# First level of a sum over eight shifts by accumulating DMA, in a pre-layernorm block with local dilated attention and a gated ReLU feed-forward

## Chip, cores and metric

One core of one Trainium2 chip. The metric is device time in microseconds (us) of one execution. Before the change it is 209.4 us, the median of 13 runs (208.21 to 209.86).

TensorE (PE) multiplies matrices into PSUM, VectorE (DVE) does elementwise work, ScalarE (ACT) does activations and copies out of PSUM. GpSimd (POOL) and SyncE (SP) can issue DMAs. Each engine takes its instructions in the order in which they were written: one that waits holds up all behind it on that engine.

## What is computed

`x` is 2048 rows by 512, in bf16. Cut to what matters:

```python
# attention: 32 heads of 16; row s sees rows s, s-2, ..., s-14
qkv = layernorm(x) @ wqkv
logits[s, w] = (q[s] . k[s - 2*w]) * scale        # w = 0..7, masked where s - 2*w < 0
attn = softmax(logits over w)
o[s] = sum over w of attn[s, w] * v[s - 2*w]
h = x + o @ wo
# feed-forward, F = 1376
n = layernorm(h)
out = h + (relu(n @ W_gate) * (n @ W_up)) @ W_down
```

## The kernel before

Everything is held transposed where it can be: the 512 features on 4 x 128 partitions, the rows along the free axis. The 2048 rows are cut into four **chunks** of 512 (`tk` = 0 to 3), and each chunk goes through the same stages.

1. *First layernorm*: statistics on DVE (L390, L393), logarithm and exponential for the reciprocal root on ACT, then four normalized `row` tiles. The table `LNA` says which engine makes them: for chunk 0 DVE (L425), for chunks 1, 2 and 3 ACT (L422), which needs one small DVE step more (L411). PE transposes them (L456), ACT copies them out (L470).
2. *Projections* q, k, v: L502 on PE, copied out by ACT (L510).
3. *Scores*: products of q with four shifted views of k at a time on DVE (L549, four a chunk, 128x4096 each), summed over each head by PE (L555); exponential on ACT (L571), denominator (L588) and its reciprocal (L591, L594), each weight spread over the partitions of its head by PE (L616) and copied out by ACT (L622) into a `big` tile of 8 x 512 columns. In chunks 1 to 3 the weights are normalized before this (L603), in chunk 0 at the end (L644).
4. *Weighted sum*: for each of the four feature groups `t`, DVE multiplies the spread weights by eight shifted views of v into a `big` tile (L637) and adds the eight shifts in a tree of three levels: 4 + 4, then 2 + 2 (both L640), then 1 + 1 (L640 in chunk 0, L663 in the others).
5. *Output projection*: L683 on PE, and the residual. For chunk 0 (`RPE = (0,)`) PE adds x through an identity matmul (L686), and ACT copies the sum out with a row total (L692). For the other chunks DVE adds it (L694).
6. *Second layernorm* (L352, L360, L400, L407, L425), transposes as above, then *feed-forward*: up and gate matmuls (L721), copies (L725, L728), their product on DVE (L741), the down projection (L758), residual (L769) and the output DMA (L773).

The stages of different chunks overlap. Their order is not that of the loops: every step is given to a small planner (`Plan`) with an engine, a duration, what it depends on and the buffers that it takes. `order()` repeatedly looks, on each engine, at the steps that could start first by those durations (within a margin of 0.3 us on DVE), and takes the one with the smallest number in the table `RANK`. The steps are then written out in order of planned start. `RANK` is a hand-kept list with one number for each step.

Buffers that the weighted sum shares: five `big` tiles serve the score products, the spread weights and the trees; nine `quad` tiles hold transposed rows; eight PSUM banks serve everything that PE writes.

After the setup GpSimd has nothing to do. Input and weight DMAs go from SP and ACT, output DMAs from SP.

Of the kernel before, what the change touches and what calls it, by code (L numbers as in the profile page):

```python
# [13 lines left out]
ALU = mybir.AluOpType  # L14
# [1 line left out]


RANK = [
    4, 1, 5, 2, 0, 3, 47, 6, 7, 29, 171, 229, 201, 272, 727, 10, 12, 8, 11, 14,
    17, 23, 28, 32, 20, 26, 31, 16, 18, 21, 24, 27, 34, 37, 9, 13, 15, 19, 22, 25,  # L20
    30, 33, 35, 40, 45, 42, 46, 57, 38, 43, 49, 52, 56, 61, 59, 66, 70, 78, 63, 68,
    67, 74, 75, 99, 84, 157, 136, 167, 73, 180, 72, 94, 88, 101, 109, 114, 65, 83, 87, 95,
    102, 122, 165, 209, 212, 121, 131, 129, 149, 127, 134, 144, 139, 153, 151, 156, 179, 210, 222, 226,
    164, 174, 196, 206, 224, 169, 183, 200, 216, 219, 187, 202, 208, 213, 218, 237, 247, 240, 249, 230,
    238, 233, 239, 254, 267, 255, 263, 242, 258, 243, 260, 270, 273, 282, 292, 276, 283, 295, 278, 286,
    280, 287, 291, 310, 320, 319, 327, 313, 323, 316, 324, 331, 308, 333, 302, 329, 305, 332, 299, 318,
    336, 345, 361, 352, 364, 337, 360, 330, 356, 366, 328, 351, 335, 353, 342, 354, 322, 349, 359, 358,
    381, 368, 389, 363, 384, 365, 387, 393, 355, 391, 348, 382, 399, 395, 417, 709, 733, 429, 434, 716,
    736, 371, 403, 706, 732, 406, 413, 714, 735, 44, 51, 36, 50, 39, 48, 41, 53, 55, 60, 64,
    76, 81, 71, 80, 86, 82, 85, 69, 77, 89, 105, 112, 97, 107, 108, 116, 96, 104, 125, 133,  # L30
    130, 137, 128, 135, 113, 126, 143, 344, 161, 271, 140, 338, 154, 312, 124, 141, 146, 152, 192, 132,
    147, 150, 163, 195, 205, 234, 245, 264, 252, 296, 306, 301, 307, 304, 265, 284, 300, 288, 298, 350,
    362, 370, 374, 309, 321, 339, 347, 340, 367, 372, 376, 314, 326, 334, 377, 386, 397, 390, 402, 383,
    388, 380, 385, 401, 404, 405, 407, 396, 400, 392, 398, 410, 414, 420, 426, 416, 422, 430, 419, 423,
    424, 427, 432, 440, 467, 455, 476, 454, 471, 464, 480, 486, 449, 463, 437, 457, 441, 460, 448, 461,
    466, 468, 481, 439, 465, 472, 484, 451, 469, 489, 446, 473, 458, 487, 443, 477, 462, 488, 491, 475,
    501, 479, 502, 485, 507, 482, 504, 525, 492, 512, 490, 508, 528, 495, 531, 718, 737, 521, 550, 722,
    740, 516, 535, 720, 738, 547, 552, 724, 741, 62, 90, 58, 92, 54, 91, 79, 93, 98, 100, 110,
    155, 159, 145, 158, 162, 142, 148, 119, 138, 160, 198, 220, 181, 217, 176, 214, 184, 223, 166, 228,
    172, 232, 170, 231, 186, 236, 189, 444, 173, 456, 203, 379, 168, 450, 235, 244, 259, 268, 315, 227,  # L40
    256, 257, 279, 317, 325, 343, 346, 357, 409, 369, 408, 418, 411, 394, 412, 428, 436, 435, 425, 447,
    478, 494, 498, 459, 470, 493, 497, 438, 442, 445, 452, 453, 474, 483, 496, 500, 505, 511, 519, 503,
    510, 506, 515, 509, 513, 522, 523, 514, 517, 518, 520, 527, 532, 537, 541, 538, 544, 549, 542, 545,
    534, 539, 551, 585, 606, 554, 583, 572, 603, 569, 600, 612, 564, 579, 568, 581, 555, 575, 560, 576,
    584, 574, 595, 570, 594, 562, 598, 566, 591, 602, 559, 588, 578, 608, 557, 586, 601, 611, 614, 589,
    624, 605, 636, 596, 621, 593, 619, 639, 580, 641, 610, 643, 648, 625, 655, 729, 745, 615, 650, 726,
    742, 637, 654, 728, 743, 633, 657, 730, 746, 111, 118, 106, 117, 115, 123, 103, 120, 175, 177, 178,
    190, 197, 185, 193, 204, 188, 194, 182, 191, 199, 248, 262, 211, 250, 207, 241, 215, 253, 221, 275,
    274, 290, 225, 277, 246, 281, 289, 499, 251, 556, 261, 565, 269, 561, 266, 294, 293, 341, 375, 285,
    303, 297, 311, 373, 378, 415, 421, 431, 524, 433, 530, 533, 536, 526, 529, 540, 548, 546, 543, 553,  # L50
    573, 582, 590, 558, 577, 587, 597, 567, 592, 599, 607, 563, 571, 604, 609, 620, 631, 613, 618, 616,
    623, 617, 628, 634, 635, 622, 626, 627, 629, 630, 632, 638, 640, 651, 652, 645, 649, 656, 642, 646,
    644, 647, 653, 662, 676, 658, 670, 667, 679, 660, 673, 690, 674, 693, 688, 696, 668, 681, 664, 683,
    699, 669, 692, 672, 687, 685, 689, 680, 686, 697, 665, 678, 677, 684, 661, 675, 659, 671, 694, 663,
    701, 666, 703, 682, 710, 691, 705, 712, 695, 704, 698, 708, 711, 707, 717, 734, 749, 700, 719, 739,
    750, 702, 715, 731, 747, 713, 721, 744, 751, 723, 725, 748, 752,
]


# [33 lines left out]
class Plan:  # L93
# [9 lines left out]
    def add(self, key, *a, **k):  # L103
        op = Op(*a, **k)
        op.key = key
        op.seq = len(self.ops)
        if RANK:
            op.prio = RANK[op.seq]
        self.ops.append(op)
        for b in set(op.take) | set(op.use):  # L110
            b.left += 1
        return op
# [57 lines left out]
def kernel(  # L170
# [11 lines left out]
    nc = tc.nc  # L182
# [121 lines left out]
    add = plan.add  # L304


    PESUM = ()
    NWARM = 48
    DMAT = ()

    EARLY = (1, 2, 3)

    RPE, OPE = (0,), ()

    MERGE = ()

    BCN = 4

    LNA = ((0, 1, 1, 1), (0, 0, 0, 0))


    MM, TP = 0.2165, 0.07
# [155 lines left out]
    def f_warm(wb=wb):  # L478
        for _ in range(NWARM):
            nc.tensor.matmul(wb.t[:, 0:P], lhsT=warm[:], rhs=warm[:], start=True, stop=True)  # L480
# [4 lines left out]
    for tk in range(NCK):  # L485
# [143 lines left out]
        for t in range(NT):  # L629
            mt = Buf(big_s)  # L630
            tpr = apr + 3 + t

            def f_mu(t=t, ab=ab, mt=mt, s0=s0):
                vb = vT[:, t, PADL + s0: PADL + s0 + CS]
                v8 = bass.AP(tensor=vb.tensor, offset=vb.offset,
                             ap=[list(vb.ap[0]), [-DIL, W]] + [list(y) for y in vb.ap[1:]])
                V.tensor_tensor(out=mt.t[:], in0=ab.t[:], in1=v8, op=ALU.mult)  # L637

            def f_a(n, mt):
                V.tensor_tensor(out=mt.t[:, 0:n, :], in0=mt.t[:, 0:n, :], in1=mt.t[:, n:2 * n, :],  # L640
                                op=ALU.add)

            def f_om(t=t, mt=mt, rc=rc, OT=OT):
                V.tensor_tensor(out=OT.t[:, t, :], in0=mt.t[:, 0, :], in1=rc.t[:], op=ALU.mult)  # L644

            m = add(("mu%d" % t, tk), "DVE", D40, f_mu, abd + [vd[t], kdone.get(("v", tk - 1, t))], tpr,
                    take=[mt], use=[ab], lat=DL)
            if (tk, t) in PESUM:
                u = Buf(od_s)

                def f_ac(mt=mt, u=u):
                    for w in range(W):
                        nc.tensor.matmul(u.t[:], lhsT=identity[:], rhs=mt.t[:, w, :],
                                         start=(w == 0), stop=(w == W - 1))

                def f_om(t=t, u=u, rc=rc, OT=OT):
                    V.tensor_tensor(out=OT.t[:, t, :], in0=u.t[:], in1=rc.t[:], op=ALU.mult)

                m = add(("ac%d" % t, tk), "PE", 8 * MM, f_ac, [m], tpr, take=[u], use=[mt], lat=PEL)
                oev[t] = add(("om%d" % t, tk), "DVE", D5, f_om, [m, rcd], tpr, take=[OT], use=[u, rc], lat=DL)  # L660
                continue
            def f_al(t=t, mt=mt, OT=OT):
                V.tensor_tensor(out=OT.t[:, t, :], in0=mt.t[:, 0, :], in1=mt.t[:, 1, :], op=ALU.add)  # L663

            for n, du in ((4, D20), (2, D10), (1, D2)):
                f = lambda n=n, mt=mt, f=f_a: f(n, mt)
                if n == 1 and tk in EARLY:
                    oev[t] = add(("tree%d" % t, tk), "DVE", du, f_al, [m], tpr, take=[OT], use=[mt], lat=DL)
                else:
                    m = add(("tree%d" % t, tk), "DVE", du, f, [m], tpr, use=[mt], lat=0.03)  # L670
            if tk not in EARLY:
                oev[t] = add(("om%d" % t, tk), "DVE", D2, f_om, [m, rcd], tpr, take=[OT], use=[mt, rc], lat=DL)
# [37 lines left out]
        for f0 in range(0, NFT, 2):  # L710
# [3 lines left out]
            for ft in fts:  # L714
# [20 lines left out]
                d = add(("ge%d" % (f0 // 2), tk), "ACT", A5, f_ge, [c], pr - 200, take=[gr], use=[gm], lat=AL)  # L735
                eds += [b, d]
                gts[ft] = gt
            n, fs = len(fts), P if fts[-1] < NFF else FTAIL
# [12 lines left out]
        for n, (j, c0, c1) in enumerate(parts):  # L751
# [24 lines left out]
            for lo, hi in ((0, 8), (8, NFT)):  # L776
# [3 lines left out]
                        use=[gts[ft] for ft in range(lo, hi)], lat=PEL if hi == NFT else 0.0)  # L780
# [45 lines left out]
```

The softmax here doesn't subtract the row's maximum and nothing guards it: scores larger than these inputs give would overflow.

## Time and profile before

| | |
|---|---|
| median of 13 runs | 209.4 us |
| the profiled execution | 208.21 us, of which the span from first to last instruction is 206.3 |
| granted TensorE clock | 1.000 |
| PE busy | 197.5 us |
| DVE busy | 162.3 us |
| ACT busy | 140.6 us |
| GpSimd busy | 1.8 us, all before 2.5 us |
| first level of the tree (L640, 128x2048) | 16 instructions, 1220 ns each |

All lines of profile come from one profiled execution. Engines: PE is matmul, PEld the weight load beside it. A group's line names line, engine, operation, output and inputs with their shapes, and the count; then busy us in total and the mean ns of one; then the idle time of the engine just before and what ended it. A line of the timeline gives start, length from the first to the last of a merged run, engine, line, operation and count. Neighbouring instructions of one engine overlap by some 0.08 us on DVE and more on PE, so a run of several is shorter than count times mean.

### The profile page before, as it was taken

Reading aid. Unit: us, or ns where it says so; the run is one execution under the profiler, and the core shown is the slowest. Engines: PE = TensorE matmul, PEld = TensorE weight load, DVE = VectorE, ACT = ScalarE, POOL = GpSimd, SP = SyncE. Lnnn points to the kernel's source line nnn. Section 1 sums busy time; section 2 is a strip of 40 time slices with the busy share of each in tenths; the row PEclk is TensorE's granted clock in tenths of the full one; section 3 lists DMA queues with packets and bytes.
Section 4 is the critical chain, followed back from the end, with each engine's and each line's share of the span. In section 5 each row is a group of like instructions: output and inputs, shape, how many; then the busy total and the mean of one; then the engine's idle time right before and its main releaser. Section 6 shows DMA issues by size and latency. Waiting matters only on the chain.

```text
span 206.3 us, 2992 instructions
## 1 busy us (share of the span) xinstructions
PE 197.5 (96%) x1139; PEld 97.2 (47%) x1159; DVE 162.3 (79%) x241; ACT 140.6 (68%) x277; POOL 1.8 (1%) x14
## 2 busy tenths in 40 slices
PE   8697998999999999999999999999999999999994
PEld 7563443555543344444454444454444445444452
DVE  6579999999999999998889998659998564011414
ACT  3659989989899996749588557565466553535800
POOL 3000000000000000000000000000000000000000
DMA  6999900000000000000010000001000000200003
GB/s 181 354 374 407 316 10 0 0 0 3 0 0 0 3 0 0 0 0 3 2 51 0 3 0 28 24 10 44 0 0 25 26 3 34 68 0 0 3 0 102
DMA packets 8813, 10.70 MB, mean 52 GB/s; under 512 B 512, under 2 KB 7648, under 8 KB 8800
## 3 DMA queue, kind: packets, MB, share of 16 engines
q1 hardware_dynamic: 7984, 9.73, 13.8%
q10 hardware_dynamic: 816, 0.79, 1.1%
q8 instruction: 9, 0.15, 0.3%
q14 instruction: 4, 0.03, 0.0%
HBM read 8.42 MB, written 2.10 MB: 51 GB/s over the span
## 4 chain that ended last, share of the span: by engine, by line
PE 64%; DVE 20%; issue 5%; ACT 4%; DMA 4%; SPq 1%; DVEq 0%
PE bank L721 37%; PE bank L758 19%; DVE big L549 7%; PE bank L683 5%; DVE big L637 4%; DMA x_sm<-in_A_x_dram 4%; DVE big L640 4%; DVE st L390 3%; ACT big L622 2%; PE bank L456 2%; ACT row L422 1%; PE bank L555 1%; ACT quad L510 1%; DVE quad L644 1%; PE bank L616 1%
## 5 line engine op out<-in xcount | busy, mean ns | idle before, releaser
L721 PE MATMUL bank<-quad,wu_sb 128*128 128x512 bf16 (+1 forms) x176 | 41.8, 379 | 0.1
L721 PE MATMUL bank<-quad,wg_sb 128*128 128x512 bf16 (+1 forms) x169 | 41.4, 379 | 0.3
L758 PE MATMUL bank<-wd_sb,gT 128*128 128x512 bf16 (+3 forms) x183 | 40.2, 366 | 0.2
L728 ACT ACTIVATE gr<-bank 128x512 bf16<-128x512 f32 (+1 forms) x44 | 25.8, 608 | 15.6 <-PE bank L721 10.9
L549 DVE TENSOR_TENSOR big<-quad,kT 128x4096 bf16<-128x4096 bf16 x16 | 35.9, 2283 | 0.1
L637 DVE TENSOR_TENSOR big<-big,vT 128x4096 bf16<-128x4096 bf16 x16 | 36.0, 2285 | 0.0
L725 ACT CAST up_sb<-bank 128x512 bf16<-128x512 f32 (+1 forms) x44 | 25.4, 589 | 14.3 <-PE bank L721 9.0
L640 DVE TENSOR_TENSOR big<-big 128x2048 bf16<-128x2048 bf16 (+2 forms) x36 | 30.7, 894 | 0.1
L741 DVE TENSOR_TENSOR gT<-gr,up_sb 128x1024 bf16<-128x1024 bf16 (+1 forms) x24 | 15.3, 644 | 18.3 <-ACT up_sb L725 11.6
L721 PEld LDWEIGHTS <-wg_sb 128*128 128x128 bf16 (+1 forms) x176 | 17.5, 100 | 20.6 <-issue 0.4
L721 PEld LDWEIGHTS <-wu_sb 128*128 128x128 bf16 (+1 forms) x176 | 17.5, 100 | 20.8 <-issue 0.8
L758 PEld LDWEIGHTS <-gT 128*128 128x128 bf16 (+1 forms) x187 | 17.8, 98 | 19.0 <-issue 0.9
L769 DVE TENSOR_TENSOR row<-x_sm,bank 128x512 bf16<-128x512 bf16 (+1 forms) x17 | 10.8, 654 | 9.4 <-PE bank L758 8.9
L622 ACT CAST big<-bank 128x512 bf16<-128x512 f32 x32 | 16.8, 620 | 2.1 <-PE bank L616 2.1
L470 ACT COPY quad<-bank 128x1024 bf16<-128x1024 bf16 (+1 forms) x16 | 15.2, 967 | 4.2 <-PE bank L456 3.9
L502 PE MATMUL bank<-quad,wv_sb 128*128 128x512 bf16 x61 | 15.9, 380 | 0.3 <-issue 0.2
L502 PE MATMUL bank<-quad,wq_sb 128*128 128x512 bf16 (+1 forms) x70 | 15.9, 355 | 0.1
L502 PE MATMUL bank<-quad,wk_sb 128*128 128x512 bf16 (+1 forms) x70 | 15.7, 355 | 0.1
L683 PE MATMUL bank<-wo_sb,quad 128*128 128x512 bf16 x62 | 15.0, 379 | 0.1
L360 ACT ACTIVATE row<-x_sm,mv 128x512 bf16<-128x512 bf16 x12 | 8.6, 718 | 8.1 <-DVE mv L352 7.8
L456 PE MATMUL bank<-identity,row 128*128 128x128 bf16 x128 | 10.2, 220 | 3.0 <-DVE row L425 1.9
L390 DVE BATCH_NORM_STATS2 st<-x_sm 128x6 f32<-128x512 bf16 x15 | 9.5, 681 | 3.6 <-DMA x_sm<-in_A_x_dram 3.6
(72 smaller groups left out, 165.1 us busy)
## 6 DMA issues: line engine op xcount, KB each, us to landing
out_dram<-row SPq DMA_DIRECT2D x15, 128.0 KB, 1.7
x_sm<-in_A_x_dram SPq DMA_DIRECT2D x3, 512.0 KB, 9.4
wu_sb<-in_B_W_up_dram SPq DMA_DIRECT2D x1, 1376.0 KB, 11.0
wg_sb<-in_B_W_gate_dram SPq DMA_DIRECT2D x1, 1376.0 KB, 13.4
wd_sb<-in_B_W_down_dram SPq DMA_DIRECT2D x1, 1280.0 KB, 15.7
wq_sb<-in_A_wqkv_dram SPq DMA_DIRECT2D x1, 512.0 KB, 6.3
wk_sb<-in_A_wqkv_dram ACTq DMA_DIRECT2D x1, 512.0 KB, 7.8
wv_sb<-in_A_wqkv_dram SPq DMA_DIRECT2D x1, 512.0 KB, 7.9
```

The source lines that it names most:

```text
L390: V.bn_stats(out=st.t[:], in_=x_sm[:, tk * BPC + j, :])
L502: nc.tensor.matmul(mm.t[:, lo:hi], lhsT=w3_sb[c][:, dt, t:D:NT], rhs=xnT.t[:, dt, lo:hi], start=(dt == 0), stop=(dt == NT - 1))
L549: V.tensor_tensor(out=pb.t[:].rearrange("p (t w) s -> p t w s", t=2), in0=q4, in1=k4, op=ALU.mult)
L622: nc.scalar.copy(out=ab.t[:, w, :], in_=bc.t[:])
L637: V.tensor_tensor(out=mt.t[:], in0=ab.t[:], in1=v8, op=ALU.mult)
L640: V.tensor_tensor(out=mt.t[:, 0:n, :], in0=mt.t[:, 0:n, :], in1=mt.t[:, n:2 * n, :], op=ALU.add)
L683: nc.tensor.matmul(od.t[:], lhsT=OT.t[:, t, j * P:(j + 1) * P], rhs=wo_sb[:, t, :], start=(t == 0), stop=(t == NT - 1 and tk not in RPE))
L721: nc.tensor.matmul(mm.t[:fs, :], lhsT=w_sb[:, dt, ft * P: ft * P + fs], rhs=hnT.t[:, dt, :], start=(dt == 0), stop=(dt == NT - 1))
L725: nc.scalar.copy(out=ub.t[:fs, i, :], in_=um.t[:fs, :])
L728: nc.scalar.activation(out=gr.t[:fs, i, :], in_=gm.t[:fs, :], func=ACT.Relu)
L741: V.tensor_tensor(out=gt.t[:fs, 0:n, :], in0=gr.t[:fs, 0:n, :], in1=ub.t[:fs, 0:n, :], op=ALU.mult)
L758: nc.tensor.matmul(od.t[:, c0:c1], lhsT=gts[ft].t[:fs, ft % 2, j * P:(j + 1) * P], rhs=wd_sb[:fs, ft, c0:c1], start=(ft == 0), stop=(ft == ...
```

## The change

For chunks 0, 1 and 2, each of the four trees loses its first level on DVE. In its place GpSimd issues a DMA that reads columns 4 to 7 of the `big` tile and adds them into columns 0 to 3 of the same tile, 128 partitions x 4 x 512 bf16, 512 KB each: twelve in all. The second level, on DVE, waits for that DMA. For the planner the step holds POOL for 1.5 us and lands 5.5 us after that (`DAL`). Chunk 3 keeps its first level on DVE.

Further, `RPE` becomes empty, so that the residual of chunk 0 is added on DVE (L694) as for the other chunks; L686 and L692 are not used any more. Both rows of `LNA` become zero, so that the normalized rows of chunks 1 to 3 are made by DVE (L425) and L411 and L422 are not used. `RANK` is another list of numbers throughout, three shorter for the three steps of L411.

```diff
 RANK = [
-    4, 1, 5, 2, 0, 3, 47, 6, 7, 29, 171, 229, 201, 272, 727, 10, 12, 8, 11, 14,
...
+    0, 1, 2, 3, 4, 5, 6, 7, 8, 9, 10, 11, 12, 13, 14, 15, 18, 17, 19, 22,
...
 ]
...
     PESUM = ()
+
+    DACC = tuple((k, t) for k in range(3) for t in range(4))
+    DAL = 5.5
     NWARM = 48
...
-    RPE, OPE = (0,), ()
+    RPE, OPE = (), ()
...
-    LNA = ((0, 1, 1, 1), (0, 0, 0, 0))
+    LNA = ((0, 0, 0, 0), (0, 0, 0, 0))
...
             for n, du in ((4, D20), (2, D10), (1, D2)):
                 f = lambda n=n, mt=mt, f=f_a: f(n, mt)
+                if n == 4 and (tk, t) in DACC:
+                    def f_da(mt=mt):
+                        nc.gpsimd.dma_start(mt.t[:, 0:4, :], mt.t[:, 4:8, :], accum_op=ALU.add)
+
+                    m = add(("ta%d" % t, tk), "POOL", 1.5, f_da, [m], tpr, use=[mt], lat=DAL)
+                    continue
                 if n == 1 and tk in EARLY:
                     oev[t] = add(("tree%d" % t, tk), "DVE", du, f_al, [m], tpr, take=[OT], use=[mt], lat=DL)
```

## The prediction

> **What bounds the kernel now.** I read the page's busy shares first, then busy time by stretch, the chain, and the timelines of VectorE (DVE) and TensorE (PE) around the place where chunk 0's attention hands over to its feed-forward part. The page's first part, then the busy time by stretch (length, then busy us and count for PE, weight load, DVE, ScalarE, GpSimd; granted clock, DMA share, GB/s):
>
> ```profile
> PE 197.5 (96%) x1139; PEld 97.2 (47%) x1159; DVE 162.3 (79%) x241; ACT 140.6 (68%) x277; POOL 1.8 (1%) x14
> ```
> ```profile
> 16.00:24.00 8.00, 6.73 (x58) 2.86 (x57) 8.00 (x11) 7.51 (x13) 0.00 (x0) 1.00 1.05 388
> ...
> 32.00:40.00 8.00, 7.37 (x67) 3.26 (x66) 8.00 (x5) 8.00 (x16) 0.00 (x0) 1.00 0.00 0
> 40.00:64.00 24.00, 23.89 (x132) 12.26 (x134) 24.00 (x29) 22.39 (x46) 0.00 (x0) 1.00 0.00 1
> 64.00:72.00 8.00, 7.51 (x68) 3.00 (x70) 8.00 (x9) 7.95 (x19) 0.00 (x0) 1.00 0.01 2
> 72.00:200.00 128.00, 127.32 (x644) 59.27 (x650) 93.15 (x138) 78.69 (x152) 0.00 (x0) 1.00 0.04 13
> ```
>
> PE is the bound. From 40 to 200 us it is idle for 0.11 + 0.49 + 0.68 = 1.3 us, at the full granted clock. The rest of its 8.8 idle us lies in the first 40 us and after 200. DVE is full too, but only until about 96 us; from 72 to 200 it is busy 93 of 128 us. The chain of waits says the same: before 68 us it runs over DVE and ScalarE (ACT), and after that almost wholly over PE. The order of time around the change, first DVE, then PE:
>
> ```profile
> 37.70 6.69 DVE L637 TENSOR_TENSOR big<-big,vT 128x4096 bf16<-128x4096 bf16 x3
> 44.31 1.22 DVE L640 TENSOR_TENSOR big<-big 128x2048 bf16<-128x2048 bf16 x1
> ...
> 55.55 0.75 DVE L644 TENSOR_TENSOR quad<-big,rec 128x512 bf16<-128x512 bf16 x2
> ...
> 68.14 1.38 DVE L425 TENSOR_SCALAR row<-x_sm,mv,rs 128x512 bf16<-128x512 bf16 x4
> ```
> ```profile
> 56.56 1.03 PE L683 MATMUL bank<-wo_sb,quad 128*128 128x512 bf16 x4
> 57.43 0.38 PE L686 MATMUL bank<-x_sm,identity 128*128 128x512 bf16 x1
> ...
> 69.48 1.03 PE L502 MATMUL bank<-quad,wv_sb 128*128 128x512 bf16 x4
> ...
> 72.32 1.90 PE L721 MATMUL bank<-quad,wg_sb 128*128 128x512 bf16 x7
> ```
>
> Until 72.3 us PE lives on the projections (L502) of all four chunks. The last four of these matmuls start at 69.48, and the layernorm rows that open chunk 0's feed-forward are made at 68.14. So the stock of other work runs out just as chunk 0 delivers: lateness of chunk 0 becomes PE idle time nearly one to one.
>
> **The change part by part.** Groups with shapes kept apart give the prices:
>
> ```profile
> L640 DVE TENSOR_TENSOR big<-big 128x2048 bf16<-128x2048 bf16 x16 | 19.0, 1220 | 0.0
> ...
> L422 ACT ACTIVATE row<-x_sm,nb,rs 128x512 bf16<-128x512 bf16 x12 | 9.5, 826 | 1.4 <-DVE nb L411 1.4
> ...
> L694 DVE SCALAR_TENSOR_TENSOR x_sm<-x_sm,bank 128x512 bf16<-128x512 bf16 x12 | 8.3, 688 | 3.4 <-PE bank L683 3.4
> ...
> L692 ACT ACTIVATE x_sm<-bank 128x512 bf16<-128x512 f32 x4 | 2.4, 615 | 0.0
> ...
> L686 PE MATMUL bank<-x_sm,identity 128*128 128x512 bf16 x4 | 1.5, 379 | 0.0
> ```
>
> *PE.* Four residual matmuls (L686) go. Their record says 379 ns, but the L683 groups around them start 57.64 - 56.56 = 1.08 us apart for five matmuls, 0.216 each. On a bound PE this is -0.87 us, the only certain gain.
>
> *ACT.* It loses twelve layernorm rows (L422, 12 x 0.79 busy = 9.5 us) and four residual passes with their sum reads (2.4 + 0.9). Until 64 us it is nearly full, but PE's measured waits for these rows are only 1.1 us. I credit nothing here: the rows do not vanish, they queue on DVE.
>
> *DVE.* Twelve first-level adds go, at a pitch of 1.13 us (1.22 less overlap): -13.6. It gains twelve rows at 0.345 (1.38 / 4), +4.1, and four residuals at 0.86 with sum read and mean (the pitch of L694 at 130.44 to 131.30), +3.4 less the 0.5 of means that it has already; three L411 go, -0.4. Net about -7 us, of which chunk 0 sees little, because all twelve rows are placed before its result. The rank table, read as order of preference, gives DVE from 16.06 us, where the first product (L549) can start as before: six products at 2.20, four value products (L637) at 2.20, eleven rows, five statistics at 0.62, eight aggregates at 0.1 and 0.24 of masks. That is 13.2 + 8.8 + 3.8 + 3.1 + 0.8 + 0.2 = 29.9, so the first waiting second-level add stands at 46.0. Then come its own 0.6, a row, two products, the rest of the trees (0.94 + 0.34 + 1.2 + 0.68) and four multiplications at 0.34: chunk 0's last output at 55.9, against 56.2 now. A product, four residuals with one L603 (3.8) and two products follow, so the four layernorm rows run from 66.3 to 67.7, against 68.14 to 69.5. One more product ends at 69.9, and its 0.55 us of score matmuls stand ahead of the first feed-forward matmul. PE gets there at 72.3 - 0.87 - 1.1 (two score groups now placed later) = 70.3. DVE at 70.4 and PE at 70.3 meet with nothing to spare, so the 1.7 us that DVE wins there is worth nothing.
>
> *The DMA adds.* Twelve transfers of 512 KB go from GpSimd's queue, which is otherwise empty after 2.4 us; SP's queue gets none. Each waits for its value product on DVE; DVE then waits for the landing. In chunk 0 the first product ends at 38.1 and its add is wanted at 46.0: 7.9 us are hidden by three value products, three rows and two aggregates. The others have 8.8, 11 and 8.0. Behind the waiting instruction on DVE stand the last row of chunk 3 (PE's transposes), the next products (PE's scores) and all of chunk 0's trees (PE's L683). In chunk 1 the slack is about 9.7, 8.5, 7.5 and 7.8, and in chunk 2 7.2, 7.3, 6.7 and 5.4; there DVE was idle for 3 us between 128.9 and 136, which absorbs part.
>
> No row shows such a transfer. Below: an output DMA of 128 KB lands in 1.7 us. At the best rate seen, 407 GB/s, its data need 0.3, which leaves 1.4 fixed. Two reads of 512 KB need 2.6, together 4.0. The Trainium skill ("DMA: Bandwidth & Descriptors", Anatomy of one DMA) puts a GpSimd-issued DMA at 2.0 us plus bytes over 436 GB/s; with both reads, 4.4 as an estimate. A rule speaks against it: "SBUF — State Buffer" (Who interferes with whom) says that descriptors written by GpSimd wait while VectorE holds the port pair that they share. DVE is 8.00 of 8.00 busy here, so a full block would add up to one 2.28 us instruction to each transfer: 6.7. The same section says two-input adds and products take only the read side; by that nothing is added, and only the rows (0.35) can block. No row decides, as GpSimd is silent from 2.4 us on. Above: at half the rate the first needs 1.4 + 5.2 + 2.3 = 8.9, and each later one, started 2.2 us after it, falls back by another 3.0. The nearest row is the output DMA, so I take 6 to 7: under the slack, cost nil, gain nil, because all it frees on DVE is spent on the rows. With the cover gone (landing at 10), DVE stalls 2.1 us at the first add.
>
> Sum: the profiled execution took 208.21 us (span 206.3, 1.9 around it); minus 0.87 gives 207.3. It was the fastest of the 13 runs, 1.2 under their median, so against the median the forecast is 209.4 - 0.9 = **208.5**.
>
> **The rivals.** *A, adds hidden, gain is the four matmuls:* 208.5, 207.6 to 209.4 by itself. Chance 0.45. *B, adds land late:* the wait of the second-level add takes the place of the first level. At a landing of 10 us, 2.1 - 0.9 = +1.2, so 210.6; 11 us gives 211.6. It decides from a landing of 7.9 + 0.9 = 8.8 us. For it: DVE is saturated, port lock, four transfers in a row. Against it: idle DMA engines (0.00 share at that time) and 4.0 to 6.7 from row and page. 0.30. *C, the new order costs:* the rows stand before products, and residuals behind a product, on a DVE with no idle time before 96 us. If chunk 0's layernorm rows slip behind one product more (2.2 us), PE idles that long at the meeting point; less 0.9, 210.7. 0.12. *D, ACT's relief closes gaps:* of PE's 2.4 idle us between 16 and 72 half goes, 209.4 - 0.9 - 1.2 = 207.3. 0.13. *That it does nothing* beyond moving DVE's idle time to later is A without the matmuls, inside A's range.
>
> **How the numbers follow.** A measurement of this kernel tells about 0.2% (0.4 us) from no change. Faster: D and three quarters of A, 0.46. Same: a fifth of A and some of B and C, 0.14. Slower: the rest, 0.40. The likeliest is A, 208.5. The range runs from D's 207.0 to B at a landing of 11 us, 211.6; outside lie a half-rate DMA and a full closing of gaps.
>
> **What would show it.** Right: DMA issues on GpSimd's queue land in under 7.9 us, DVE shows no wait for them in chunk 0, L686 is gone, the first L721 starts near 70.3, PE busy falls by about 0.9 to 1.5, and PE's idle time from 40 to 200 stays near 1.3. Wrong: a row in the waits in which DVE's L640 waits for a DMA for over 1 us, with PE idle before L683, L456 or L721 between 50 and 75 us; or PE waiting for rows now made on DVE.

## The result, and the profile after

The changed kernel takes 207.7 us, the median of 11 runs (205.57 to 208.44), against 209.4 in the same comparison: a ratio of 0.992, 95% interval 0.990 to 0.994, so 1.3 to 2.2 us faster. A second comparison gave 0.994 (0.991 to 0.997). The forecast was 208.5, faster by 0.9: the right sign and inside the range, but only about half of the gain.

Two profiles of each kernel are needed to read it, because the start varies. In some executions of either kernel PE waits about 1.3 us for the first projection weights, in others hardly. The early-start pair is the profile shown of before (span 206.3) and a second one of after (204.7). The late-start pair is a second profile of before (207.4) and the first of after (205.8). At equal starts the change is worth 1.6 us both times. The lines below are from the early-start profile of after unless said otherwise. First its busy shares, then busy time by stretch with the columns as before:

```profile
PE 198.1 (97%) x1155; PEld 97.1 (47%) x1155; DVE 155.2 (76%) x246; ACT 131.2 (64%) x257; POOL 12.3 (6%) x26
```
```profile
16.00:24.00 8.00, 7.49 (x57) 3.63 (x55) 8.00 (x9) 5.79 (x10) 0.00 (x0) 1.00 1.05 391
...
32.00:40.00 8.00, 8.00 (x60) 4.09 (x59) 8.00 (x9) 7.88 (x15) 1.01 (x1) 1.00 0.09 18
40.00:64.00 24.00, 24.00 (x137) 11.81 (x136) 23.96 (x38) 18.54 (x38) 2.59 (x3) 1.00 0.44 83
64.00:72.00 8.00, 7.57 (x72) 3.35 (x71) 8.00 (x9) 7.63 (x15) 0.00 (x0) 1.00 0.01 2
72.00:200.00 128.00, 128.00 (x663) 59.03 (x662) 86.64 (x133) 76.71 (x149) 6.88 (x8) 1.00 0.21 46
```

PE still sets the end. Its busy time is above the 197.5 us of before only because that profile lacks 20 matmul records (x1139 beside x1159 weight loads), and a missing one shows as a little idle time. The late-start profile of before has them all, and 198.9 us. DVE is as full until 64 us as it was, although the four adds of chunk 0 are gone: the rows took their place, as forecast. ACT is what became lighter, 18.5 us of 24 instead of 22.4. PE's idle time from 8 to 72 us fell from 2.6 to 2.0 in the early-start pair. The order of time where chunk 0 hands over, first DVE, then PE:

```profile
45.20 0.67 DVE L643 TENSOR_TENSOR big<-big 128x1024 bf16<-128x1024 bf16 x1
...
54.13 1.08 DVE L647 TENSOR_TENSOR quad<-big,rec 128x512 bf16<-128x512 bf16 x3
64.75 1.37 DVE L428 TENSOR_SCALAR row<-x_sm,mv,rs 128x512 bf16<-128x512 bf16 x4
```
```profile
54.88 1.89 PE L692 MATMUL bank<-wo_sb,quad 128*128 128x512 bf16 x8
...
64.39 1.03 PE L505 MATMUL bank<-quad,wv_sb 128*128 128x512 bf16 x4
65.90 1.07 PE L459 MATMUL bank<-identity,row 128*128 128x128 bf16 x16
68.92 1.04 PE L730 MATMUL bank<-quad,wu_sb 128*128 128x512 bf16 x4
```

The second-level add starts at 45.2 with no wait in front (forecast 46.0), and the layernorm rows at 64.75 (66.3). The first feed-forward matmul starts at 68.92 (70.3); the late-start profile has 46.2, 65.8 and 69.94. The DMA issues (the last figure is median us from issue to landing) and the only wait for them, from the waits:

```profile
big<-big POOLq DMA_DIRECT2D x12, 512.0 KB, 5.7
```
```profile
DVE big L643 <- DMA big<-big: 1.3, 1, 1.3
```

The four adds of a chunk land in nearly the same pattern each time: in chunk 0 4.6, 5.3, 6.0 and 6.3 us after issue. The issue starts 0.3 us after the product ends, or 0.5 in three of the twelve. The one wait, in the late-start profile 1.05 us, is at the last add of chunk 2, where the prediction counted the shortest slack (5.4).

Two stretches sum this up: A, from the first projection matmul to the first feed-forward matmul, which takes out the start, and B, from there to the end of the span.

| kernel (profile) | A | PE idle in A | B |
|---|---|---|---|
| before, early / late start | 64.05 / 63.89 | 2.6 / 2.0 | 134.0 / 134.0 |
| after, early / late start | 60.61 / 60.58 | 1.7 / 1.0 | 135.8 / 135.9 |
| DMA adds alone, old order | 63.3 | 2.4 | 134.0 |
| DMA adds and residual, old order | 65.3 | 4.3 | 134.1 |
| all three edits, old order | 70.3 | 6.8 | 134.1 |
| after, adds on DVE, order kept | 65.1 | 5.2 | 143.1 |
| after, residual on PE, order kept | 61.5 | 2.2 | 135.8 |
| after, rows on ACT, order kept | 65.5 | 5.5 | 135.8 |
| after, adds landing late | 62.9 | 3.5 | 135.8 |

"Old order" is what the planner makes of the old ranks when the DMA adds are in. PE's order is then that of the kernel before, but DVE's and ACT's differ from it in places.

A falls by 3.3 to 3.4, and 0.9 of this is the four matmuls. The new order also places two score groups and one L619 group in B. They take 0.55, 0.55 and 0.33 us, and each adds 0.1 to the four matmuls ahead of it, which then take 0.96 from start to start instead of 0.86:

```profile
47.49 1.03 PE L505 MATMUL bank<-quad,wk_sb 128*128 128x512 bf16 x4
48.45 0.61 PE L558 MATMUL bank<-big,sel 128*32 128x512 bf16 x8
49.00 1.05 PE L505 MATMUL bank<-quad,wq_sb 128*128 128x512 bf16 x4
```

So 1.7 us of work moved from A to B, which agrees with the rise of B by 1.8. Waiting has no part in that rise: in the two profiles that have all matmul records, PE is busy all the time from the first feed-forward matmul to 200 us. First the late-start profile of before, then the early-start one of after:

```profile
73.41:200.00 126.59, 126.59 (x644) 58.42 (x641) 92.80 (x138) 78.35 (x151) 0.00 (x0) 1.00 0.04 13
```
```profile
68.92:200.00 131.08, 131.08 (x682) 60.28 (x679) 89.72 (x134) 79.76 (x155) 6.88 (x8) 1.00 0.21 45
```

The remaining 0.7 to 0.8 us of A is PE kept better supplied. Its idle time in A fell by 0.9 (early) and 1.0 (late). This is rough: the early-start profile of before and the late-start one of after lack seven matmul records each in A.

### The profile page after: what moved, and what is told of

It is laid out like the page before. It is cut to its first block, busy times and chain, and to the rows that moved or that the text cites. A ratio compares the mean times of both kernels' runs of the same rounds, so it can differ in the third digit from the quotient of the medians.

```text
span 205.8 us, 2989 instructions
## 1 busy us (share of the span) xinstructions
PE 198.2 (96%) x1136; PEld 97.9 (48%) x1155; DVE 155.2 (75%) x246; ACT 131.6 (64%) x257; POOL 12.3 (6%) x26
## 4 chain that ended last, share of the span: by engine, by line
PE 65%; DVE 24%; DMA 5%; ACT 2%; issue 2%; SPq 1%
PE bank L730 37%; PE bank L767 18%; DVE big L552 11%; PE bank L692 5%; DMA x_sm<-in_A_x_dram 5%; DVE big L640 3%; DVE row L428 2%; DVE st L393 2%; DVE big L643 2%; PE bank L558 1%; PE bank L459 1%; ACT big L625 1%; DVE x_sm L703 1%; PE bank L619 1%; DVE quad L647 1%
## 5 line engine op out<-in xcount | busy, mean ns | idle before, releaser
L730 PE MATMUL bank<-quad,wu_sb 128*128 128x512 bf16 (+1 forms) x173 | 42.8, 379 | 0.2
L767 PE MATMUL bank<-wd_sb,gT 128*128 128x512 bf16 (+3 forms) x183 | 39.7, 366 | 0.2
L750 DVE TENSOR_TENSOR gT<-gr,up_sb 128x1024 bf16<-128x1024 bf16 (+1 forms) x24 | 15.4, 644 | 21.3 <-ACT up_sb L734 12.2
L473 ACT COPY quad<-bank 128x1024 bf16<-128x1024 bf16 (+1 forms) x16 | 14.7, 963 | 10.1 <-PE bank L459 10.1
L625 ACT CAST big<-bank 128x512 bf16<-128x512 f32 x32 | 17.6, 608 | 1.7 <-PE bank L619 1.5
L505 PE MATMUL bank<-quad,wq_sb 128*128 128x512 bf16 (+1 forms) x72 | 17.0, 373 | 1.4 <-DMA wq_sb<-in_A_wqkv_dram 1.4
L643 DVE TENSOR_TENSOR big<-big 128x1024 bf16<-128x1024 bf16 (+2 forms) x24 | 17.0, 729 | 1.1 <-DMA big<-big 1.1
L505 PE MATMUL bank<-quad,wk_sb 128*128 128x512 bf16 (+1 forms) x70 | 16.6, 367 | 0.2
L672 POOL DMA_DIRECT2D big<-big x12 | 10.5, 875 | 100.4 <-DVE big L640 75.7
L505 PE MATMUL bank<-quad,wv_sb 128*128 128x512 bf16 x61 | 15.3, 379 | 0.3 <-issue 0.2
L692 PE MATMUL bank<-wo_sb,quad 128*128 128x512 bf16 x62 | 15.2, 380 | 0.1
L513 ACT CAST kT<-bank 128x512 bf16<-128x512 f32 x16 | 9.3, 598 | 7.5 <-PE bank L505 7.2
L703 DVE SCALAR_TENSOR_TENSOR x_sm<-x_sm,bank 128x512 bf16<-128x512 bf16 x16 | 10.9, 684 | 3.6 <-PE bank L692 3.6
```

The source lines that it names most:

```text
L473: nc.scalar.copy(out=o, in_=i)
L505: nc.tensor.matmul(mm.t[:, lo:hi], lhsT=w3_sb[c][:, dt, t:D:NT], rhs=xnT.t[:, dt, lo:hi], start=(dt == 0), stop=(dt == NT - 1))
L625: nc.scalar.copy(out=ab.t[:, w, :], in_=bc.t[:])
L692: nc.tensor.matmul(od.t[:], lhsT=OT.t[:, t, j * P:(j + 1) * P], rhs=wo_sb[:, t, :], start=(t == 0), stop=(t == NT - 1 and tk not in RPE))
L730: nc.tensor.matmul(mm.t[:fs, :], lhsT=w_sb[:, dt, ft * P: ft * P + fs], rhs=hnT.t[:, dt, :], start=(dt == 0), stop=(dt == NT - 1))
L750: V.tensor_tensor(out=gt.t[:fs, 0:n, :], in0=gr.t[:fs, 0:n, :], in1=ub.t[:fs, 0:n, :], op=ALU.mult)
```

## The experiments

**Does the start explain the difference of the profiles?** The kernel before, once more.

> The kernel before once more, for a second profile. The profiled execution of before was the fastest of 13 and had its first projection matmul at 8.3 us, the changed kernel's at 9.4 with PE waiting 1.4 us for a weight load. Theory 1 (the start varies from execution to execution, and the kernel before, full on DVE until 96 us, hands a late start on to the end): a start about 1 us later and a span about 1 us longer, 207.3, with the first feed-forward matmul at 73.3. Rival (the late start belongs to the changed order): first projection matmul at 8.3 again, whatever the span.

It started late, and kept the lateness to the end. Its span was 207.4 and its time 209.32; the first projections and the first feed-forward matmuls:

```profile
9.52 1.50 PE L502 MATMUL bank<-quad,wq_sb 128*128 128x256 bf16 x12 [1.29 <-DMA wq_sb<-in_A_wqkv_dram]
...
73.41 1.90 PE L721 MATMUL bank<-quad,wg_sb 128*128 128x512 bf16 x8
```

8.27 became 9.52 and 72.32 became 73.41. So the forecast's base, the fastest of 13 runs, was an early start, and a late start comes without the change too. Theory 1 holds.

> The changed kernel once more. Theory 1: 0.990 to 0.994 of before; PE idle time between 16 and 40 us well under the 1.95 of before whatever the start. Rival (the small idle time there was only the consequence of the late start): with an early start it is near 1.5 again.

0.994 (0.991 to 0.997), at the upper end of what theory 1 gave. With an early start PE's idle time from 16 to 40 us is 0.72 (24 - 7.49 - 7.79 - 8.00) against 1.95, and with a late start 0.36 against 1.59: 1.2 less in both pairs, and the rival's 1.5 did not come. But from 8 to 16 us the early start after has 0.82 against 0.08, waits for the first weights, so the net saving from 8 to 72 is the 0.7 above.

**Undoing one part, with the planner free.** The first three runs each took one part back and let the planner order the rest by the same ranks.

```diff
-    DACC = tuple((k, t) for k in range(3) for t in range(4))
+    DACC = ()
```

> The changed kernel (207.7 us) with all its first-level adds back on DVE; rows, residuals and ranks as changed. Theory 1, the rows that DVE took over spend what the DMA adds free: four adds at 1.13 us stand ahead of chunk 0's hand-over again while the twelve rows stay there, so chunk 0 comes 4.5 us later than in the changed kernel and PE, whose stock of projections ends there, idles about 4: 211 to 212. Theory 2, DVE is not on the path and the DMA adds are worth nothing: 207.7 within 0.4.

```diff
-    RPE, OPE = (), ()
+    RPE, OPE = (0,), ()
```

> The changed kernel with chunk 0's residual back on PE and ACT. Theory 1, the gain is the four matmuls: 0.87 us slower than the changed kernel, 208.6. Rival: DVE's four residuals (2.9 us) behind a product cost what the matmuls win, since DVE and PE meet with nothing to spare: 207.7 or faster.

```diff
-    LNA = ((0, 0, 0, 0), (0, 0, 0, 0))
+    LNA = ((0, 1, 1, 1), (0, 0, 0, 0))
```

> The changed kernel with the twelve normalized rows of chunks 1 to 3 back on ACT (three small DVE steps more, each placed right after the exponential before it). Theory 1 (the prediction: ACT's relief is worth nothing, the rows cost DVE 4.1 us ahead of the hand-over): 207.7 or up to 1 us faster. Rival (ACT's relief is what closed PE's idle time between 16 and 40 us, 1.95 us in the profile before and 0.36 after): slower by 1 to 1.6, 208.7 to 209.3, with the PE waits for ACT's rows back.

All three overshot every expectation: 1.043 (1.039 to 1.047), 1.040 (1.036 to 1.044) and 1.047 (1.043 to 1.051), 8 to 10 us over the kernel before. With the residual on PE, stretch A was only 61.2, but B was 144.8: PE waited 4.5 us for normalized rows of later chunks, and after the longest of these waits (3.03 us) the granted clock was 0.50 from 113.0 to 119.9 us. A changed engine or duration moves planned starts, and with the same ranks the planner picks another order. Each was therefore run again with the plan left as it was and only the emitted instructions changed. For the residual the order was most of the loss, and for the rows about half: with the order kept they are 9 and 6 us faster than here. For the adds it was not: 218.5 here, 219.5 with the order kept.

**The adds on DVE, order kept.**

```diff
                     def f_da(mt=mt):
-                        nc.gpsimd.dma_start(mt.t[:, 0:4, :], mt.t[:, 4:8, :], accum_op=ALU.add)
+                        V.tensor_tensor(out=mt.t[:, 0:4, :], in0=mt.t[:, 0:4, :], in1=mt.t[:, 4:8, :], op=ALU.add)
```

> The changed kernel with each DMA add replaced, at its place in the order, by the add on DVE; every engine's order is otherwise that of the changed kernel, which the run with the adds back on DVE did not keep. Theory 1 (the adds pay for the rows on DVE): four adds of 1.13 us ahead of the hand-over of chunk 0, first feed-forward matmul at 74 to 75 instead of 69.9, and 211 to 213 in all. Theory 2 (DVE off the path): 207.7 within 0.4.

219.5 us, 1.050 (1.046 to 1.054). Stretch A grew by 4.5, as much as four adds at 1.13. B grew by another 7.3, which neither theory had. The timeline of PE shows two of the places, and the waits what it waited for:

```profile
51.27 0.62 PE L459 MATMUL bank<-identity,row 128*128 128x128 bf16 x8 [3.11 <-DVE row L428]
...
92.50 1.89 PE L730 MATMUL bank<-quad,wg_sb 128*128 128x512 bf16 x8 [1.48 <-ACT gr L737]
```
```profile
PE bank L730 <- ACT gr L737: 4.7, 3, 2.3
PE bank L459 <- DVE row L428: 3.9, 3, 3.1
```

The adds of chunk 1 (L672) stand on DVE ahead of the gate product (L750), and ACT's next copy waits for that product:

```profile
90.00 1.22 DVE L672 TENSOR_TENSOR big<-big 128x2048 bf16<-128x2048 bf16 x1
91.14 0.68 DVE L750 TENSOR_TENSOR gT<-gr,up_sb 128x1024 bf16<-128x1024 bf16 x1
...
91.85 0.60 ACT L737 ACTIVATE gr<-bank 128x512 bf16<-128x512 f32 x1 [3.85 <-DVE gT L750]
```

The product comes late, so the buffers of ACT's copies are not free, ACT's copies are late, PSUM banks stay full and PE stops. Part of the 7.3 is a granted clock of 0.50 from 97.9 to 101.3 us, around the longest of these stops (2.34 us). In the changed order the twelve DMA adds carry twelve microseconds. That is not what they are worth against the kernel before, whose order was made for adds on DVE.

**The residual of chunk 0 on PE and ACT, order kept.**

```diff
+    EPE = (0,)
-                                     start=(t == 0), stop=(t == NT - 1 and tk not in RPE))
-                if tk in RPE:
+                                     start=(t == 0), stop=(t == NT - 1 and tk not in EPE))
+                if tk in EPE:
```

> The changed kernel with chunk 0's residual on PE and ACT, order otherwise kept. Theory 1 (the four matmuls are the gain): 0.87 us slower than the changed kernel, 208.6, first feed-forward matmul 0.9 to 1.0 later. Rival (the four residuals on DVE cost as much as the matmuls): 207.7 or faster, since DVE is 2.9 us lighter at the hand-over.

209.0 us, 0.999 (0.997 to 1.002). Stretch A grew by 0.93, the four matmuls at 0.216 and little else. By the ratios the loss is 0.999 - 0.992, 1.6 us, with some 0.7 of uncertainty from the two intervals together; 0.87 is at its lower edge, and the changed kernel's second comparison (0.994) makes the loss 1.2. The rival is out: DVE was idle for 3.2 us between 40 and 64 us (24 - 20.84 busy) and it bought nothing.

**The rows on ACT, order kept.**

```diff
-                if on_act:
+                if not residual and tk:
+                    if not made:
+                        made.append(f_nb(lo, hi))
                     nc.scalar.activation(out=xn.t[:], in_=x, func=ACT.Identity,
```

> The changed kernel with the twelve rows of chunks 1 to 3 made by ACT at the same places in the order, each set behind its small DVE step. Theory 1 (the prediction: worth nothing): 207.7 within 0.5, DVE being 3.7 us lighter before the hand-over. Rival (ACT's relief closes PE's gaps before 40 us): 1 to 3 us slower, with PE idle in front of the transposes and projections between 16 and 40 us.

213.1 us, 1.019 (1.016 to 1.023). The 5.0 to 5.8 us against the changed kernel are more than the rival said, and 4.9 of them lie in A. Busy time by stretch:

```profile
16.00:24.00 8.00, 6.60 (x48) 3.46 (x47) 6.25 (x7) 6.89 (x14) 0.00 (x0) 1.00 1.04 390
24.00:32.00 8.00, 7.24 (x53) 2.98 (x52) 7.66 (x13) 6.64 (x13) 0.00 (x0) 1.00 0.25 80
32.00:40.00 8.00, 6.03 (x42) 2.90 (x40) 4.81 (x7) 8.00 (x16) 0.00 (x0) 1.00 0.01 3
```

With the rows in its queue ACT is late with everything behind them. DVE, lighter by the rows, is idle for 5.3 us of these 24, and PE for 4.1. In the kernel before, whose ACT order was made for it, the same load cost PE only 1.1 us of waits for rows. So ACT's relief was worth something, and this run bounds it from above, not as its worth.

**The DMA adds alone on the kernel before.** The lines of `DACC`, `DAL` and `f_da` from the diff of the change, without its other parts. The planner was free here: on DVE a score product now stands ahead of chunk 0's last tree.

> The kernel before with the twelve DMA adds alone; its ranks, rows on ACT and residual on PE as before. Theory 1 (PE's stock of projections ends at 72 us whatever DVE does, so DVE's 4.5 us are spent on waiting): 209.4 within 0.5. Rival (the adds are the gain of the change by themselves): 207.7 to 208.3.

208.3 us, 0.996 (0.993 to 0.998): a gain of 0.9 us (0.5 to 1.4), at the rival's upper edge and outside theory 1. The two comparisons of the whole change gave 1.7 and 1.3, so all its other parts together add 0.4 to 0.8, little more than the noise. A is 63.3, 0.6 less than in the late-start profile of before. First the wait at the hand-over in the early-start profile of before; then, in this run, the rows there and PE's start after it:

```profile
68.60 1.04 PE L456 MATMUL bank<-identity,row 128*128 128x128 bf16 x12 [0.27 <-DVE row L425]
```
```profile
66.86 1.38 DVE L428 TENSOR_SCALAR row<-x_sm,mv,rs 128x512 bf16<-128x512 bf16 x4
```
```profile
72.59 1.89 PE L730 MATMUL bank<-quad,wg_sb 128*128 128x512 bf16 x7 [0.30 <-ACT quad L473]
```

Although this profile started a microsecond late, the rows come 1.3 us earlier than in the early-start profile of before (68.14). PE's wait for them (0.27 in both profiles of before) is gone, and its idle time from 64 to 72 us is 0.06, where it was 0.49 (early) and 0.27 (late). So in the kernel before DVE was on PE's path at the hand-over, by up to half a microsecond.

**DMA adds and the residual on DVE, old order.** As the last, with L686 and L692 gone and L694 used for chunk 0.

> The kernel before with the twelve DMA adds and chunk 0's residual on DVE instead of PE and ACT; rows of chunks 1 to 3 stay on ACT, order that of the run with the DMA adds alone (208.3, 0.9956). Theory 1 (matmuls worth 0.87): 207.4, about as fast as the changed kernel, so the rows add nothing. Rival (DVE's residuals behind products cost the matmuls' gain): 208.3.

210.9 us, 1.010 (1.006 to 1.013), a miss for both. The matmuls are saved, but the residuals now queue on DVE behind products of chunk 2 (one of them starts at 64.88), the second layernorm comes late, and PE idles 1.8 us from 64 to 72. **All three edits, old order:**

> All three edits of the change (DMA adds, residual and rows on DVE) in the order of the kernel before: the run with DMA adds and residual (210.9), with the twelve rows on DVE at the places that ACT had for them. Theory 1 (the rows on DVE relieve ACT and close PE's gaps before 40 us): faster than 210.9 by 1 to 3, 208 to 210, and what remains to 207.7 is the new rank list. Rival (DVE pays 4.1 us for them before the hand-over): slower than 210.9, 212 to 215.

215.6 us, 1.029 (1.026 to 1.032): the rival, and 0.6 past its range. PE's waits:

```profile
PE bank L463 <- DVE row L432: 6.1, 4, 2.1
```

At the places that ACT had for them, the rows wait behind 2.2-us products on DVE, and PE's transposes wait for the rows. From the longest of these waits on the granted clock was 0.50, from 20.7 to 27.5 us, which is part of the loss. In the old order the three edits are 6 us slower than the kernel before and 8 slower than the changed kernel: they are a gain only with a rank list that moves the rows in between the products. What the new list would give without the edits was not run.

**Adds that land late.** Copies that change no result, queued ahead of chunk 0's first add, and one extra add at the end, on a tile no longer needed.

```diff
+                        if (tk, t) == (0, 1):
+                            for i in range(3):
+                                nc.gpsimd.dma_start(scr[i], mt.t[:, 4:8, :])
                         nc.gpsimd.dma_start(mt.t[:, 0:4, :], mt.t[:, 4:8, :], accum_op=ALU.add)
...
+                    V.tensor_copy(out=bt[:, 4, 0:2], in_=gt.t[:, 0, 0:2])
+                    nc.gpsimd.dma_start(bt[:, 0:4, :], bt[:, 4:8, :], accum_op=ALU.add)
```

> The changed kernel with three plain copies of 512 KB from SBUF to HBM queued on GpSimd ahead of chunk 0's first add, whose data nobody reads, and one more add at about 184 us, when DVE is idle, on a tile no longer needed. Theory 1 (the prediction's rival B: the slack is 7.6 to 8 us from product to second level and then time is lost one to one): copies of about 1.3 us each put the landings at 8.7 to 10.2 us, DVE waits 2 to 3 us in chunk 0, 2 to 3 us slower than the changed kernel, about 210. Rival (other slack takes it up): under 0.5 slower. For the late add: if DVE's use of the shared port holds back the descriptors it lands clearly sooner than the 4.5 us of a first add beside a full DVE, 3.5 or less; if not, 4.4 to 4.7.

210.2 us, 1.003 (1.002 to 1.005); against the changed kernel 2.1 to 2.5 us slower. DVE's waits in chunk 0 and the first feed-forward matmul:

```profile
46.70 0.69 DVE L644 TENSOR_TENSOR big<-big 128x1024 bf16<-128x1024 bf16 x1 [1.39 <-DMA big<-big]
...
54.80 1.96 DVE L644 TENSOR_TENSOR big<-big 128x1024 bf16<-128x1024 bf16 x4 [0.95 <-DMA big<-big]
```
```profile
71.48 1.04 PE L734 MATMUL bank<-quad,wu_sb 128*128 128x512 bf16 x4
```

1.39 + 0.95 = 2.3 us of waiting make stretch A 2.3 longer (62.9): one to one, as rival B had it. The adds landed 7.0 to 10.1 us after issue. The late add was issued at 194.3 us and landed after 5.4, with DVE busy for 0.7 us of that time and no output DMA issued between 180 us and its landing. That is no sooner than the 4.5 beside a full DVE, so it gives no sign that DVE holds the descriptors back. Why it took longer than 4.5 stays open.

## Why the prediction was right, and where its size was off

*PE is the bound and DVE meets it with nothing to spare:* right, and shown from both sides. 2.3 us more waiting on DVE is 2.3 us more in A; DVE made lighter (residual on PE) gains nothing.

*Four matmuls, 0.87:* right; 0.93 in A.

*The placing on DVE:* the sum by hand came within a microsecond of both profiles for the first two places (46.0 for 45.2 and 46.2; 55.9 for 55.2 and 56.2). The layernorm rows came earlier than the 66.3 of the sum, by 1.6 and 0.5 us (64.75 and 65.8). PE came earlier as well (68.92 for 70.3), in part because the moved work was 1.7 us and not 1.1; what moves from A to B changes nothing in the total.

*The adds land in 6 to 7 us, hidden:* right; 5.0 to 7.4 from the end of the product. The rule on the shared port (the Trainium skill, "SBUF — State Buffer", Who interferes with whom) would have added up to one 2.28-us instruction to each, 6.7 from issue. A first add's 4.5 to 4.6 beside a DVE that is busy all the time agrees with its other half, which the page marks as inferred, that two-input instructions take only the read side. What lengthens the later ones is their own queue: each takes 0.2 to 0.9 us longer than the one before, and where the adds alone issue one 5.1 us after the last (chunk 1), it lands in 4.5 again.

*"Gain nil, because all it frees on DVE is spent on the rows":* right for the changed kernel at the hand-over, where the prediction looked. PE's idle time from 64 to 72 us is 0.43 (early) and 0.50 (late) after the change, against 0.49 and 0.27 before, and at 68.38 it waits 0.43 us for a product of DVE. Without the rows on DVE the same adds do free PE there (0.06) and gain 0.9 us. So the adds pay for the rows.

*"ACT: I credit nothing here":* this is the term that was mis-sized. PE's waits for ACT's rows in the early-start profile of before:

```profile
PE bank L456 <- ACT row L422: 1.1, 2, 0.8
```

They are gone in both profiles of after, and between 16 and 72 us PE never waits for a row that DVE makes. This is about the 0.7 to 0.8 us by which A fell beyond matmuls and moved work. The prediction had the effect as rival D, with half of 2.4 us, and gave the sum without it; the result lies between A and D. That the relief of ACT is the cause is read from these waits and not shown by a run of its own: the rows on DVE were a gain only together with the adds and the new order.

*PE's idle time from 40 to 200 us, "near 1.3":* it did stay, but at another size. The two profiles with all matmul records have 0.43 before and 0.43 after; most of the rest of the 1.3 was missing records.

*Rival C, the order costs:* it did not happen, but it was the larger risk. The same edits in the old order are 6 us slower than before, and any single part undone with free planning 8 to 10.

No run here is faster than the changed kernel; the adds alone, at 208.3 us, come nearest.

## What to carry to other kernels

Where one engine is the bound and a hand-kept order feeds it, an edit on another engine is worth little or much according to where its instructions stand. Undo a part with the order frozen, or the run measures the new order too. Even then the order was made for the part, so the loss bounds its worth from above. Compare stretches that begin and end at an event of the bounding engine, which takes out a start that varies by more than the effect. A DMA that replaces a compute step has to be checked against the slack of each of its places, counted in the instructions that stand between, with its own queue added when several follow each other.

## What the runs showed of the hardware

An accumulating DMA of 512 KB from SBUF to SBUF costs GpSimd 0.86 us of issue. It landed 4.5 to 4.6 us after issue as the first of a chunk (5.4 in the one late case), and when issued every 2.2 us each took 0.2 to 0.9 longer than the last. Two output DMAs of 128 KB issued beside the last add of chunk 2 took 5.5 and 6.2 us to land in the early-start profile, where the median is 1.7; adds issued close to such a pair took 6.6 to 8.0. In the late-start profile the DMA engines were 80% busy for the 14 us that hold the four adds of chunk 0, so one occupies them for 0.8 x 14 / 4 = 2.8 us. That is 187 GB/s of destination, less than half of the 407 seen for loads. DVE's products beside it kept their 2.28 us.

The granted clock fell to 0.50 for 3.4 or 6.8 us in some executions. In the late-start profile of after this lasted from 9.1 to 12.5 us, around a PE wait of 1.43 us for weights, and four 256-column matmuls took 1.04 us where the early start has 0.63. The late-start profile of before kept 1.00 through a wait of 1.29. The length of the wait does not decide it alone: with the adds on DVE and the order kept, a wait of 3.11 us at 51.27 left 1.00, and one of 2.34 us at 98.50 stands in a stretch of 0.50. What decides it was not tried.
